# Another issue order, paired first q matmuls and PSUM places written out in a fused attention, FFT and MLP kernel

## The chip, the cores and the metric

The kernel runs on one core of a Trainium2 chip. The time is device microseconds of that core from the start of a launch to its end, the median of several executions. Every execution starts with all inputs in HBM, the weights among them as 64-bit patterns that the kernel decodes itself.

## What is computed

The reference, cut to what matters (four batches, four heads, sequence 1088, head dimension 32, r = 8, so 64 features):

```python
def phi(x):                                   # S1, S2: (8, 32)
    a = einsum('rd,bhsd->bhsr', S1, x)
    b = einsum('rd,bhsd->bhsr', S2, x)
    return einsum('bhsi,bhsj->bhsij', a, b).reshape(..., 64)
kv  = einsum('bhsf,bhsd->bhfd', phi(k), v);  z = sum(phi(k), axis=s)
x   = einsum('bhsf,bhfd->bhsd', phi(q), kv) / (einsum('bhsf,bhf->bhs', phi(q), z) + 1e-6)
u   = x + real(fft(fft(x, axis=seq), axis=channel))       # x as (4, 1088, 128)
un  = (u - mean(u)) / sqrt(var(u) + 1e-6)                 # over the 128 channels
y   = u + relu(un @ w_ch1) @ w_ch2                        # 128 -> 512 -> 128
h   = relu(y @ w_in)                                      # 128 -> 1024
out = (h * sigmoid(conv3(h))) @ w_out                     # 3 taps along the sequence
```

## The kernel before

The channels (or four heads times 32) lie on the 128 partitions, the sequence on the free axis. Each of the four batches goes through five stages: `load_attn`, `attn`, `fft`, `moe1` (normalization and the first MLP) and `moe2` (the second). The code is written stage by stage, but no instruction is issued where it stands: `Program` records each call, and `issue` (line 153) sends them out in the order of the table `ORDER`, so that batches and stages overlap and each engine's queue is fixed by the table. All profile lines carry the line number of the recorder (L157) for that reason, and groups are told apart by their tiles. No scheduler reorders anything after that; an instruction waits in its engine's queue for the semaphores of its operands.

What the change and the steps of the prediction touch:

- `load64` (line 182) loads a 64-bit weight (`raw`) on SP's queue and decodes it: one ACT operation and six on DVE, on the tile `em`. It is called for `srep` (the two 8x32 matrices S1, S2), `w1`, `w2`, `win` in two halves, `cw` and `wout` in two halves.
- From `s_rep` come `sab_sb` (eight DVE copies, weights for the factors `a` and `b`) and `sq_sb` (eight ACT copies, the same with each row repeated eight times).
- `idle` (line 235): 24 matmuls on zeros that write a tile nobody reads. Each fp32 matmul makes two records in the trace, so 24 are 48 records.
- `consts_fft` (line 274): `mats_sb` on SP's queue; `tab_hi`, `tab_lo`, `tab_end` (2.6 MB of cosines and sines) on POOL's queue, each behind a one-column copy that reads `q_sb[0]`, so that no table is fetched before the first q is there.
- `attn`: for batch 0 (`P["sq"]`) the features of q come from 12 matmuls of 128 rows by 364 columns against `sq_sb`, an ACT copy and a DVE product for each two. The other batches take `qab_ps<-q,sab_sb` (4 matmuls), and spread the result through DRAM. For k: 9 matmuls `kab_ps`, a copy `kb`, six products `kp` on DVE. Then `kv_ps`: 36 matmuls that write one of two column halves (`kp_0` the one, `kp_1` the other), an ACT copy `vk` for each half and one transposing matmul `kvt_ps` (batches 0, 1, 3: `P["kvt"]`), or 18 matmuls `kv_ps<-v,kp` that need no transposing (batch 2). `kv` and `z` are copied out of PSUM by DVE (lines 404, 405). `den` (24 matmuls of 32 columns), its reciprocal `rd`, and `num` (6) follow; batch 0 spreads `rd` by the matmuls `rb`.
- `fft`: `xe` and `xo` (even and odd part), four DVE operations `parts`, the matmuls `p_ps`, then `spec` against the tables.
- `q_sb`, `k_sb` and `v_sb` have one buffer each, so the load of batch 1's q waits for the last matmul that reads batch 0's.
- PSUM: `bank` gives a tile of one bank from one of two pools, five banks for `mm` and three for `acc`.

Of the kernel before, what the change touches and what calls it, by code (L numbers as in the profile page):

```python
# [9 lines left out]
F32 = mybir.dt.float32  # L10
# [5 lines left out]
ALU = mybir.AluOpType  # L16
# [3 lines left out]
P = dict(near=(0,), kvt=(0, 1, 3), hs=(), hlo=4, xb=2, sq=(0,), rpe=(0,), up=(0,), mo=12, hid=7, idle=24)  # L20
BANKS = {"mm": 5, "acc": 3}
# [8 lines left out]
HALF = 544  # L30
RT = 273
# [107 lines left out]
class Program:  # L139
# [13 lines left out]
    def issue(self):  # L153
        assert sorted(ORDER) == list(range(len(self.ops)))
        for i in ORDER:
            fn, args, kw = self.ops[i]
            fn(*args, **kw)  # L157
# [576 lines left out]
```

## Time and profile before

| | us |
|---|---|
| median of 3 executions | 260.36 (259.74 to 261.38) |
| profiled execution, span of its instructions | 259.4 |
| median minus that span | 0.96 |
| PE busy | 250.8 (97%) |
| DVE busy | 234.4 (90%) |
| ACT busy | 183.6 (71%) |

The profiled execution's own time is known by its span, from the first to the last instruction on the core. Busy shares are over that span. PE's busy time counts a matmul until its modelled end, and matmuls overlap, so that 97% means that PE is nearly always given work and not that it could do none in less time. In the chain that ended last PE has 81% of the span, DVE 10%, transfers 4%.

### The profile page before, as it was taken

Reading aid. Unit: us, or ns where it says so; the run is one execution under the profiler, and the core shown is the slowest. Engines: PE = TensorE matmul, PEld = TensorE weight load, DVE = VectorE, ACT = ScalarE, POOL = GpSimd, SP = SyncE. Lnnn points to the kernel's source line nnn. Section 1 sums busy time; section 2 is a strip of 40 time slices with the busy share of each in tenths; the row PEclk is TensorE's granted clock in tenths of the full one; section 3 lists DMA queues with packets and bytes.
Section 4 is the critical chain, followed back from the end, with each engine's and each line's share of the span. In section 5 each row is a group of like instructions: output and inputs, shape, how many; then the busy total and the mean of one; then the engine's idle time right before and its main releaser. Section 6 shows DMA issues by size and latency. Waiting matters only on the chain.

```text
span 259.4 us, 4622 instructions
## 1 busy us (share of the span) xinstructions
PE 250.8 (97%) x1812; PEld 198.5 (77%) x1812; DVE 234.4 (90%) x356; ACT 183.6 (71%) x330; POOL 6.5 (2%) x15
## 2 busy tenths in 40 slices
PE   7799999999999999999989999999999999999994
PEld 7566679876979887778878877678988877877652
DVE  2588999988999999989999999999999998999970
ACT  3342433972986847873788978996999998999822
POOL 1400000030000000000000000000000000000000
PEclk9799999999999999999999999999999999999999
DMA  7999299385568204184303001500000050000202
GB/s 225 329 402 284 85 304 236 115 228 179 123 147 195 75 24 122 42 175 131 86 4 114 11 0 15 137 0 0 3 0 29 9 143 0 0 3 1 85 0 86
DMA packets 11557, 26.87 MB, mean 104 GB/s; under 512 B 2224, under 2 KB 6832, under 8 KB 11280
## 3 DMA queue, kind: packets, MB, share of 16 engines
q1 hardware_dynamic: 11136, 23.92, 32.9%
q0 software_dynamic: 400, 2.67, 2.9%
q8 instruction: 14, 0.23, 0.4%
q14 instruction: 7, 0.06, 0.1%
HBM read 23.27 MB, written 3.31 MB: 102 GB/s over the span
## 4 chain that ended last, share of the span: by engine, by line
PE 81%; DVE 10%; DMA 4%; ACT 2%; issue 1%; SPq 0%; ACTq 0%; DVEq 0%
PE z L157 25%; PE acc L157 20%; PE ch L157 10%; PE qab_ps L157 5%; DMA q<-qT 4%; PE spec L157 4%; PE kv_ps L157 4%; DVE t L157 4%; PE p_ps L157 3%; PE num L157 3%; PE kab_ps L157 2%; PE cen L157 2%; ACT t L157 1%; PE var L157 1%; DVE ch L157 1%
## 5 line engine op out<-in xcount | busy, mean ns | idle before, releaser
L157 DVE SCALAR_TENSOR_TENSOR t<-h,cw_sb,t 128x1087 f32<-128x1087 f32 x64 | 83.8, 1340 | 0.9 <-ACT t L157 0.4
L157 PE MATMUL acc<-t,wo_sb 128*128 128x364 f32 (+1 forms) x192 | 69.3, 469 | 0.0
L157 ACT ACTIVATE h<-z 128x364 f32<-128x364 f32 (+1 forms) x96 | 41.0, 472 | 15.2 <-PE z L157 14.8
L157 DVE TENSOR_TENSOR t<-t,h 128x1088 f32<-128x1088 f32 (+2 forms) x34 | 40.9, 1217 | 4.6 <-ACT t L157 4.5
L157 PEld LDWEIGHTS acc<-t,wo_sb 128*128 128x128 f32 x192 | 34.3, 189 | 9.1 <-DVE t L157 0.6
L157 ACT ACTIVATE t<-h,cw_sb 128x1088 f32<-128x1088 f32 x32 | 38.4, 1204 | 0.4
L157 ACT ACTIVATE t<-t 128x1088 f32<-128x1088 f32 (+2 forms) x34 | 35.5, 1058 | 4.3 <-DVE t L157 4.3
L157 PE MATMUL z<-yh,win_hi 128*128 128x364 f32 (+1 forms) x96 | 37.2, 414 | 0.0
L157 PE MATMUL z<-yl,win_hi 128*128 128x364 f32 (+1 forms) x96 | 34.1, 366 | 0.2 <-DVE yl L157 0.2
L157 PE MATMUL z<-yh,win_lo 128*128 128x364 f32 (+1 forms) x96 | 34.1, 359 | 0.0
L157 PE MATMUL ch<-hid,w_sb 128*128 128x364 f32 (+1 forms) x96 | 33.3, 469 | 0.0
L157 ACT ACTIVATE hid<-z 128x364 f32<-128x364 f32 (+1 forms) x48 | 21.3, 474 | 7.4 <-PE z L157 7.1
L157 PEld LDWEIGHTS ch<-hid,w_sb 128*128 128x128 f32 x96 | 17.3, 189 | 6.6 <-ACT hid L157 0.5
L157 PEld LDWEIGHTS z<-yh,win_hi 128*128 128x128 f32 x96 | 17.7, 189 | 5.1 <-ACT h L157 1.0
L157 PEld LDWEIGHTS z<-yh,win_lo 128*128 128x128 f32 x96 | 18.1, 189 | 3.1
L157 PEld LDWEIGHTS z<-yl,win_hi 128*128 128x128 f32 x96 | 18.0, 189 | 2.6 <-DVE yl L157 0.5
L157 PE MATMUL z<-uh,w_hi 128*128 128x364 f32 (+1 forms) x48 | 19.2, 410 | 0.0
L157 PE MATMUL z<-uh,w_lo 128*128 128x364 f32 (+1 forms) x48 | 16.9, 358 | 0.0
L157 PE MATMUL z<-ul,w_hi 128*128 128x364 f32 (+1 forms) x48 | 16.4, 359 | 0.0
L157 PE MATMUL p_ps<-mats_sb,parts 128*32 128x128 f32 (+1 forms) x160 | 15.4, 276 | 0.7 <-ACT pe L157 0.7
L157 PEld LDWEIGHTS p_ps<-mats_sb,parts 128*32 128x32 f32 (+1 forms) x160 | 13.2, 142 | 2.2 <-ACT pe L157 0.9
L157 DVE TENSOR_TENSOR kp<-kab_ps,kb 121x512 f32<-121x512 f32 (+1 forms) x24 | 12.2, 546 | 0.5 <-ACT kb L157 0.5
(118 smaller groups left out, 389.3 us busy)
## 6 DMA issues: line engine op xcount, KB each, us to landing
qa<-qd SPq DMA_DIRECT2D x6, 546.0 KB
qb<-qd SPq DMA_DIRECT2D x12, 273.0 KB
v<-va SPq DMA_DIRECT2D x4, 594.0 KB
q<-qT SPq DMA_DIRECT2D x4, 546.0 KB, 6.4
k<-kT SPq DMA_DIRECT2D x4, 544.5 KB
x<-rrd SPq DMA_DIRECT2D x12, 136.5 KB, 4.1
y<-rtd SPq DMA_DIRECT2D x3, 544.0 KB
out<-r SPq DMA_DIRECT2D x8, 182.0 KB
```

The lines of the kernel that those rows point to most:

```text
L157: fn(*args, **kw)
```

## The change

It has six parts. (1) SP's queue starts with `srep`, q and k of batch 0, and `w1` comes behind them; the second half of `win` is fetched ahead of the first; POOL's copies that hold the tables back read `v_sb[0]` in place of `q_sb[0]`. (2) Batch 0's q features: 12 matmuls of 64 rows each in place of 12 of 128 rows (the other 64 rows of those weights are zeros); row halves 0 and 64 take turns, and the matmuls of a pair write different banks. (3) All eight PSUM banks are one tile `every`, and `HOMES` says for each use which bank it has; the 12 `wide` slots get written-out places too. (4) Batch 2 takes the transposed form of kv too. (5) The copies of `kv` and `z` go from DVE to ACT (16 instructions). (6) `xe` and `xo` become one tile `xeo`, and the four `parts` operations of a batch two. `idle` goes from 24 to 15 matmuls, all of them ahead of the first q matmul. And the whole table `ORDER` is another one.

```diff
-P = dict(near=(0,), kvt=(0, 1, 3), ..., sq=(0,), rpe=(0,), up=(0,), mo=12, hid=7, idle=24)
-BANKS = {"mm": 5, "acc": 3}
+P = dict(near=(0,), kvt=(0, 1, 2, 3), ..., sq=(0,), rpe=(0,), up=(0,), mo=12, hid=7, idle=15)
...
-    def bank(nm, tag="mm"):
-        return ps.tile([128, 512], F32, tag=tag, bufs=BANKS[tag], name=nm)
+    every = ps.tile([128, 8, 512], F32, name="every") if HOMES else None
+    def bank(nm):
...
+        return every[:, int(next(homes["bank"]))]
...
         for t, src in ((tab_hi, thi), (tab_lo, tlo), (tab_end, tend)):
-            G.tensor_copy(t[:, 0, 0:1], q_sb[0][:t.shape[0], 0:1])
+            G.tensor_copy(t[:, 0, 0:1], v_sb[0].rearrange("p t h d -> p (t h d)")[:t.shape[0], 0:1])
             G.dma_start(t, src)
...
-            for hp in range(2):
-                for i in range(3):
-                    c = slice(i * 364, (i + 1) * 364)
-                    pab = [bank(f"qab_ps{b}_{hp}_{i}_{s}", "acc") for s in range(2)]
-                    for s in range(2):
-                        w = sq_sb[:, s, 2 * hp:2 * hp + 2].rearrange("p h i j -> p (h i j)")
-                        T.matmul(pab[s][:, :364], w, qt[:, c], start=True, stop=True)
+            for i in range(3):
+                c = slice(i * 364, (i + 1) * 364)
+                pab = {}
+                for s in range(2):
+                    for hp in range(2):
+                        r = slice(64 * hp, 64 * hp + 64)
+                        w = sq_sb[r, s, 2 * hp:2 * hp + 2].rearrange("p h i j -> p (h i j)")
+                        pab[s, hp] = bank(f"qab_ps{b}_{hp}_{i}_{s}")
+                        T.matmul(pab[s, hp][:, :364], w, qt[r, c], start=True, stop=True)
...
-            V.tensor_copy(kv[r, :, 32 * h2:32 * h2 + 32], kvv[h2][:, :, 0:32])
-            V.tensor_copy(zz[r, ...], kvv[h2][:, :, 32])
+            A.copy(kv[r, :, 32 * h2:32 * h2 + 32], kvv[h2][:, :, 0:32])
+            A.copy(zz[r, ...], kvv[h2][:, :, 32])
...
-        for i, (src, op, eng) in enumerate(
-            ((xe, ALU.add, V), (xe, ALU.subtract, V), (xo, ALU.subtract, V), (xo, ALU.add, V))
-        ):
-            eng.tensor_tensor(parts[:, i], src[:, 0:RT], src[:, HALF:RT - 2:-1], op=op)
+        for to, op in ((parts[:, 0:4:3], ALU.add), (parts[:, 1:3], ALU.subtract)):
+            V.tensor_tensor(to, xeo[:, :, 0:RT], xeo[:, :, HALF:RT - 2:-1], op=op)
```

The first place where the order differs is SP's queue at the start. `raw` is a weight's buffer, `q0`, `k0`, `v0` are batch 0's inputs, `q1`, `k1` batch 1's. Before:

```order
L157 DMA raw0_110<-w1 128x512
L157 DMA raw0_78<-srep 128x16
L157 DMA q0_109<-qT 128x1092
L157 DMA k0_107<-kT 128x1089
L157 DMA raw0_115<-win 128x512
L157 DMA mats_sb_93<-mats 128x896
L157 DMA v0_108<-va 128x1188
L157 DMA raw0_113<-w2 128x512
L157 DMA k1_258<-kT 128x1089
L157 DMA q1_260<-qT 128x1092
```

Now:

```order
L164 DMA raw0_79<-srep 128x16
L164 DMA q0_109<-qT 128x1092
L164 DMA k0_107<-kT 128x1089
L164 DMA raw0_110<-w1 128x512
L164 DMA mats_sb_93<-mats 128x896
L164 DMA raw512_116<-win 128x512
L164 DMA v0_108<-va 128x1188
L164 DMA q1_181<-qT 128x1092
L164 DMA raw0_112<-w2 128x512
L164 DMA k1_179<-kT 128x1089
```

`w1` has gone from the first place to the fourth, the other half of `win` stands there, and batch 1's q has come ahead of `w2` and of its k.

The second place is PE's queue at the start, up to the first `kv` matmuls. Before, where the tiles `qab_ps`, `kab_ps` and `kv_ps` have names of their own:

```order
L157 MATMUL idle_88<-still_87 128x128 x13
L157 MATMUL qab_ps0_0_0_0_134<-q0_109,sq_sb_81 128x364
L157 MATMUL qab_ps0_1_0_0_140<-q0_109,sq_sb_81 128x364
L157 MATMUL kab_ps0_0_128<-sab_sb_80,k0_107 121x64 x5
L157 MATMUL qab_ps0_1_0_1_141<-q0_109,sq_sb_81 128x364
L157 MATMUL qab_ps0_1_1_0_142<-q0_109,sq_sb_81 128x364
L157 MATMUL kab_ps0_0_128<-sab_sb_80,k0_107 121x64 x3
L157 MATMUL qab_ps0_0_1_0_136<-q0_109,sq_sb_81 128x364
L157 MATMUL qab_ps0_0_2_0_138<-q0_109,sq_sb_81 128x364
L157 MATMUL kab_ps0_1_129<-sab_sb_80,k0_107 121x64
L157 MATMUL qab_ps0_0_1_1_137<-q0_109,sq_sb_81 128x364
L157 MATMUL qab_ps0_1_2_0_144<-q0_109,sq_sb_81 128x364
```

Now, where every result is a bank of `every` and the operands tell what a row is (`q0,sq_sb` the features of q, `sab_sb,k0` those of k, `q1,sab_sb` batch 1's q, `kp0,v0` batch 0's kv):

```order
L164 MATMUL every_75<-still_88 128x128 x15
L164 MATMUL every_75<-q0_109,sq_sb_82 128x364 x12
L164 MATMUL every_75<-sab_sb_81,k0_107 121x64 x9
L164 MATMUL every_75<-em0_111,mats_sb_93 128x512
L164 MATMUL every_75<-q1_181,sab_sb_81 64x273
L164 MATMUL every_75<-kp0_0_127,v0_108 33x64 x14
L164 MATMUL every_75<-q1_181,sab_sb_81 64x273
L164 MATMUL every_75<-kp0_0_127,v0_108 33x64 x4
L164 MATMUL every_75<-kp0_1_128,v0_108 33x64 x18
L164 MATMUL every_75<-q1_181,sab_sb_81 64x273
```

The q matmuls stand in one row of twelve, the nine of k behind them; batch 1's q has come ahead of the kv matmuls, and those stand in runs, 18 of `kp0_0` (14 and 4) and then 18 of `kp0_1`, where before the two take turns.

The third place is batch 1's kv on PE. Before, a part of it (the pattern goes on to the end):

```order
L157 MATMUL kv_ps1_274<-kp1_0_272,v1_259 33x64
L157 MATMUL kv_ps1_274<-kp1_1_273,v1_259 33x64
L157 MATMUL kv_ps1_274<-kp1_0_272,v1_259 33x64
L157 MATMUL kv_ps1_274<-kp1_1_273,v1_259 33x64 x2
L157 MATMUL kv_ps1_274<-kp1_0_272,v1_259 33x64
L157 MATMUL kv_ps1_274<-kp1_1_273,v1_259 33x64
```

Now, between the last `spec` matmuls of batch 0 and its `moe1`:

```order
L164 MATMUL every_75<-kp1_1_190,v1_180 33x64
L164 MATMUL every_75<-q2_245,sab_sb_81 64x273
L164 MATMUL every_75<-kp1_1_190,v1_180 33x64 x3
L164 MATMUL every_75<-q2_245,sab_sb_81 64x273
L164 MATMUL every_75<-kp1_0_189,v1_180 33x64 x2
L164 MATMUL every_75<-kp1_1_190,v1_180 33x64 x6
L164 MATMUL every_75<-q2_245,sab_sb_81 64x273
L164 MATMUL every_75<-kp1_0_189,v1_180 33x64
L164 MATMUL every_75<-kp1_1_190,v1_180 33x64 x4
L164 MATMUL every_75<-q2_245,sab_sb_81 64x273
L164 MATMUL every_75<-kp1_0_189,v1_180 33x64 x15
L164 MATMUL every_75<-kp1_1_190,v1_180 33x64 x4
```

The halves stand in runs of up to 15 here, with batch 2's q (`q2`) in between. Over batches 1 to 3, 76 of the 108 kv matmuls follow one of the same half, where before it is 11 of 72 (batch 2 had the other form).

On DVE, the decode of `win`'s first half (`em0_115`) and the end of that of `w2` have gone from ahead of batch 0's `xe` and `parts` to behind its `spec`. The matmuls that wait for PE's own semaphore were 15 and are none.

## Rows read from the trace of the kernel before

**Rows 1.** The page's head and part 1: busy time, share, instructions.
```profile
span 259.4 us, 4622 instructions
...
PE 250.8 (97%) x1812; PEld 198.5 (77%) x1812; DVE 234.4 (90%) x356; ACT 183.6 (71%) x330; POOL 6.5 (2%) x15
```

**Rows 2.** Windows: width, busy us by engine (count), clock, DMA.
```profile
0.00:40.00 40.00, 35.81 (x325) 26.98 (x326) 29.99 (x81) 15.78 (x41) 3.71 (x11) 0.96 0.82 272
40.00:250.00 210.00, 209.12 (x1471) 168.23 (x1470) 202.82 (x273) 166.01 (x287) 2.75 (x4) 1.00 0.28 74
```

**Rows 3.** Timeline of the first 40 us: start, length, engine, instruction, idle before it.
```profile
0.72 0.40 SPq L157 DMA_DIRECT2D raw<-w  x1
...
1.17 4.97 PE L157 MATMUL idle<-still 128*128 128x128 f32 x26 [1.17 <-DVE still L157]
1.19 0.41 SPq L157 DMA_DIRECT2D raw<-srep  x1
...
4.71 0.77 ACT L157 ACTIVATE em<-raw 128x16 f32<-128x16 f32 x2 [2.71 <-DMA raw<-srep]
...
6.00 0.18 DVE L157 TENSOR_TENSOR s_rep<-em 128x16 f32<-128x16 f32 x1
...
6.27 1.52 ACT L157 COPY sq_sb<-s_rep 32x64 f32<-32x64 f32 x6 [0.79 <-DVE s_rep L157]
...
8.17 1.34 PE L157 MATMUL qab_ps<-q,sq_sb 128*128 128x364 f32 x2 [2.03 <-DMA q<-qT]
...
12.15 1.44 PE L157 MATMUL qab_ps<-q,sq_sb 128*128 128x364 f32 x4
...
14.62 1.88 DVE L157 TENSOR_TENSOR kp<-kab_ps,kb 121x512 f32<-121x512 f32 x3 [0.47 <-ACT kb L157]
...
22.57 0.30 PE L157 MATMUL kv_ps<-kp,v 121*33 121x64 f32 x2 [0.35 <-ACT vk L157]
...
24.97 1.17 PE L157 MATMUL den<-qa,z 128*32 128x91 f32 x48
...
28.70 0.69 DVE L157 SCALAR_TENSOR_TENSOR em<-raw,em 128x512 f32<-128x512 uint32 x1
...
31.60 2.12 PE L157 MATMUL kab_ps<-sab_sb,k 128*121 128x64 f32 x18
...
34.35 1.14 PE L157 MATMUL qab_ps<-q,sab_sb 128*64 128x273 f32 x8 [0.64 <-DMA q<-qT]
...
38.86 0.39 PE L157 MATMUL spec<-tab_hi,ph 128*128 128x274 f32 x1
```

**Rows 4.** Windows of 2 us round the first `q` matmuls.
```profile
8.00:10.00 2.00, 1.83 (x4) 1.06 (x5) 1.90 (x7) 0.45 (x1) 1.57 (x4) 0.60 0.84 262
10.00:12.00 2.00, 2.00 (x11) 1.72 (x10) 0.43 (x2) 0.71 (x3) 1.42 (x3) 0.55 1.07 411
12.00:14.00 2.00, 2.00 (x14) 1.53 (x13) 0.98 (x2) 0.37 (x1) 0.00 (x0) 1.00 1.02 410
```

**Rows 5.** PE timeline, `kv_ps` in its two forms.
```profile
44.02 2.21 PE L157 MATMUL kv_ps<-kp,v 121*33 121x64 f32 x72
...
69.68 1.45 PE L157 MATMUL kv_ps<-v,kp 121*128 121x66 f32 x12
```

**Rows 6.** PE timeline at 120 us: five `kv_ps` records of one half.
```profile
120.20 0.44 PE L157 MATMUL kv_ps<-kp,v 121*33 121x64 f32 x5
```

**Rows 7.** Groups by line and form: count, busy us, mean ns, idle before.
```profile
L157 PE MATMUL kv_ps<-kp,v 121*33 121x64 f32 x216 | 8.0, 220 | 0.3 <-ACT vk L157 0.3
...
L157 DVE COPY kv<-kvt_ps 64x64 f32<-64x64 f32 x6 | 1.3, 217 | 0.1
```

**Rows 8.** DMA issues: count, KB each, median us from issue to landing.
```profile
q<-qT SPq DMA_DIRECT2D x4, 546.0 KB, 6.4
...
tab_end<-tend POOLq DMA_DIRECT2D x1, 411.0 KB, 13.9
...
rtd<-rt SPq DMA_DIRECT2D x3, 34.0 KB, 1.5
```

More of the change, by code (lines that the diff above doesn't have):

```diff
@@ L18 @@
 DRAM = bass.MemoryType.DRAM
-P = dict(near=(0,), kvt=(0, 1, 3), hs=(), hlo=4, xb=2, sq=(0,), rpe=(0,), up=(0,), mo=12, hid=7, idle=24)
-BANKS = {"mm": 5, "acc": 3}
+P = dict(near=(0,), kvt=(0, 1, 2, 3), hs=(), hlo=4, xb=2, sq=(0,), rpe=(0,), up=(0,), mo=12, hid=7, idle=15)
 LEAST, MOST = np.array([896 << 20, (1151 << 20) - 1], np.int32).view(np.float32).tolist()
@@ L47 @@
 ORDER = [
[74 rows of a table removed]
-]
[74 rows of a table added]
+]
+HOMES = {
+    "bank": (
+        "064557205141037623552734101354301031414143402555472001264327104137567232532507174722313014560546474454373746755643604777"
+        "536454432363231346156574656607457030274331235232515661553176135162555126332351064366557736361256322150236133443524550721"
+        "2403500305642450432034502422"
+    ),
+    "wide": "012391948a175b8324107a2685475046b24b751980a36255b704a62781b5097134639a6a94519a42859b043978",
+}
 class Queue:
@@ L153, in issue @@
     def issue(self):
-        assert sorted(ORDER) == list(range(len(self.ops)))
-        for i in ORDER:
+        assert not ORDER or sorted(ORDER) == list(range(len(self.ops)))
+        for i in ORDER or range(len(self.ops)):
             fn, args, kw = self.ops[i]
@@ L168, in tile_fwd, with place @@
     ln = ctx.enter_context(tc.tile_pool(name="ln", bufs=1))
-    mo = ctx.enter_context(tc.tile_pool(name="mo", bufs=P["mo"]))
+    mo = ctx.enter_context(tc.tile_pool(name="mo", bufs=1))
     dr = ctx.enter_context(tc.tile_pool(name="dr", bufs=2, space=DRAM))
-    ps = ctx.enter_context(tc.tile_pool(name="ps", bufs=5, space=PSUM))
-    def bank(nm, tag="mm"):
-        return ps.tile([128, 512], F32, tag=tag, bufs=BANKS[tag], name=nm)
+    ps = ctx.enter_context(tc.tile_pool(name="ps", bufs=1, space=PSUM))
+    homes = {kind: iter(places) for kind, places in HOMES.items()}
+    def place(pool, shape, dtype, kind, bufs, nm):
+        if kind in homes:
+            return pool.tile(shape, dtype, tag=kind + next(homes[kind]), bufs=1, name=nm)
+        return pool.tile(shape, dtype, tag=kind, bufs=bufs, name=nm)
+    every = ps.tile([128, 8, 512], F32, name="every") if HOMES else None
+    def bank(nm):
+        if every is None:
+            return ps.tile([128, 512], F32, tag="bank", bufs=8, name=nm)
+        return every[:, int(next(homes["bank"]))]
     def lo_of(eng, dst, src, hi):
@@ L179, in slot @@
     def slot(nm):
-        return mo.tile([128, WIDE], F32, tag="wide", name=nm)
+        return place(mo, [128, WIDE], F32, "wide", P["mo"], nm)
     def load64(src, n, use, then=lambda o, w, x: None):
@@ L235, in tile_fwd @@
     if P["idle"]:
-        idle = bank("idle", "acc")
+        idle = bank("idle")
         for i in range(P["idle"]):
@@ L314, in attn @@
             for i in range(2):
-                p = bank(f"qab_ps{b}_{i}", "mm")
+                p = bank(f"qab_ps{b}_{i}")
                 for j in range(2):
@@ L332, in attn @@
         kb = at.tile([KT, NKT, NH, RK], F32, tag="kb", name=f"kb{b}")
-        kp0 = bank(f"kab_ps{b}_0", "mm")
-        kp1 = bank(f"kab_ps{b}_1", "mm")
+        kp0 = bank(f"kab_ps{b}_0")
+        kp1 = bank(f"kab_ps{b}_1")
         for t in range(NKT):
@@ L360, in attn @@
         kv, zz = kvz[b % 2]
-        kv_ps = bank(f"kv_ps{b}", "mm")
+        kv_ps = bank(f"kv_ps{b}")
         if b in P["kvt"]:
@@ L376, in attn @@
                 A.copy(vk[r, :], kv_ps[r, :128])
-            kv_ps = bank(f"kvt_ps{b}", "mm")
+            kv_ps = bank(f"kvt_ps{b}")
             T.matmul(kv_ps[:, :128], vk, eye_sb, start=True, stop=True)
@@ L392, in attn @@
         if b in P["sq"]:
-            for hp in range(2):
-                for i in range(3):
-                    c = slice(i * 364, (i + 1) * 364)
-                    pab = [bank(f"qab_ps{b}_{hp}_{i}_{s}", "acc") for s in range(2)]
-                    for s in range(2):
-                        w = sq_sb[:, s, 2 * hp:2 * hp + 2].rearrange("p h i j -> p (h i j)")
-                        T.matmul(pab[s][:, :364], w, qt[:, c], start=True, stop=True)
-                    A.copy(qa[hp][:, c], pab[0][:, :364])
-                    V.tensor_tensor(qa[hp][:, c], qa[hp][:, c], pab[1][:, :364], op=ALU.mult)
+            for i in range(3):
[7 more added lines that the diff above has]
+                        T.matmul(pab[s, hp][:, :364], w, qt[r, c], start=True, stop=True)
+                for hp in range(2):
+                    A.copy(qa[hp][:, c], pab[0, hp][:, :364])
+                    V.tensor_tensor(qa[hp][:, c], qa[hp][:, c], pab[1, hp][:, :364], op=ALU.mult)
         for h2 in range(2):
             r = slice(64 * h2, 64 * h2 + 64)
-            V.tensor_copy(kv[r, :, 32 * h2:32 * h2 + 32], kvv[h2][:, :, 0:32])
-            V.tensor_copy(zz[r, DJ - 1 + DJ * h2:DJ + DJ * h2 + ZW + 2 * DJ:ZW + 2 * DJ], kvv[h2][:, :, 32])
+            A.copy(kv[r, :, 32 * h2:32 * h2 + 32], kvv[h2][:, :, 0:32])
+            A.copy(zz[r, DJ - 1 + DJ * h2:DJ + DJ * h2 + ZW + 2 * DJ:ZW + 2 * DJ], kvv[h2][:, :, 32])
         for hp in range(0 if b in P["sq"] else 2):
             V.tensor_tensor(qa[hp], qa[hp], qb[hp], op=ALU.mult)
-        den = bank(f"den{b}", "mm")
+        den = bank(f"den{b}")
         for hp in range(2):
@@ L427, in attn @@
             for c in range(4):
-                p = bank(f"rb{b}_{c}", "mm")
+                p = bank(f"rb{b}_{c}")
                 for j in range(DJ):
@@ L439, in attn @@
         for i in range(3):
-            n = bank(f"num{b}_{i}", "mm")
+            n = bank(f"num{b}_{i}")
             for hp in range(2):
@@ L453, in fft @@
         x = xs.pop(b)
-        xe = ff.tile([128, HALF + 1], F32, tag="xe", name=f"xe{b}")
-        xo = ff.tile([128, HALF + 1], F32, tag="xo", name=f"xo{b}")
+        xeo = ff.tile([128, 2, HALF + 1], F32, tag="xeo", name=f"xeo{b}")
         fw, bw = x[:, 0:HALF + 1], x[:, SEQ:HALF - 1:-1]
-        V.tensor_tensor(xe, fw, bw, op=ALU.add)
-        V.tensor_tensor(xo, fw, bw, op=ALU.subtract)
+        V.tensor_tensor(xeo[:, 0], fw, bw, op=ALU.add)
+        V.tensor_tensor(xeo[:, 1], fw, bw, op=ALU.subtract)
         parts = ff.tile([128, 4, RT], F32, tag="parts", name=f"parts{b}")
-        for i, (src, op, eng) in enumerate(
-            ((xe, ALU.add, V), (xe, ALU.subtract, V), (xo, ALU.subtract, V), (xo, ALU.add, V))
-        ):
-            eng.tensor_tensor(parts[:, i], src[:, 0:RT], src[:, HALF:RT - 2:-1], op=op)
+        for to, op in ((parts[:, 0:4:3], ALU.add), (parts[:, 1:3], ALU.subtract)):
+            V.tensor_tensor(to, xeo[:, :, 0:RT], xeo[:, :, HALF:RT - 2:-1], op=op)
         ph = ff.tile([128, 8, D], F32R, tag="ph", name=f"ph{b}")
@@ L588, in moe2 @@
         yh, yl = ys.pop(b)
-        acc = [bank(f"acc{b}_{i}", "acc") for i in range(3)]
+        acc = [bank(f"acc{b}_{i}") for i in range(3)]
         hs, ts = {}, {}
```

148 rows, old and new, of the table ORDER are left out of this document.

## The prediction

> **What bounds the kernel now.** I read the page's busy shares first: PE 97% and DVE 90% of 259.4 us [rows 1]. A share over the whole span hides stages, so the windows came next [rows 2]. From 40 to 250 us PE is busy 209.12 of 210 us and DVE 202.82: PE gives the pace, DVE follows close behind, and a gain there must take work off PE's queue without adding to DVE's. From 0 to 40 us it is otherwise: PE is busy 35.81 us, but part of that is work on zeros and part ran at a low clock. So the timeline of that stretch was read, link by link, for what the first `spec` at 38.86 us waits for [rows 3]. The chain is: the DMA of `srep`, on which ACT sat idle 2.71 us until 4.71; `s_rep` at 6.00; the `sq_sb` copies from 6.27; the first q matmul at 8.17, in front of which PE idled 2.03 us for q; the matmuls of q and k; the `kp` products from 14.62 (0.63 us each for the long ones); the last kv matmuls at 22.57; `den` at 24.97; `spec` at 38.86. In the windows behind the 2.03 us gap the granted clock is 0.60 and 0.55, so TensorE ran partly at its lower level of 1.2 GHz there, and 1.00 (2.4 GHz) from 12 us on [rows 4].
>
> **The start, step by step.** All steps are set against the profiled execution; the median lies 0.96 us above its span (260.36 against 259.4).
>
> *srep first.* Before, its DMA is issued at 1.19 us behind `w1` and ACT starts on it at 4.71, 3.5 us later [rows 3]. Issued in `w1`'s place at 0.72 it is used by 4.2 us if it takes as long; without 512 KB ahead of it less, with the 1.5 us that the 34 KB of `rtd` take [rows 8] as the other end, so 2.2. I take 2.6, near that end, since nothing stands ahead of it now. From there to the end of `s_rep` it is 1.47 us (4.71 to 6.18), and eight `sq_sb` copies at 0.25 us (six took 1.52) end at 6.2. q is issued at 1.65 and lands after 6.4 us [rows 8], so at 8.05; issued 0.46 us earlier and with 512 KB less ahead (1.25 us at the 411 GB/s of rows 4) it lands at 6.3 or before.
>
> *The clock.* 15 `idle` matmuls are 30 records; 26 took 4.97 us, from 1.17 [rows 3], so 30 end near 6.6. The q matmuls then follow with no gap: first q at 6.6 rather than 8.17, and the 3.83 busy us of the windows at 0.60 and 0.55 become some 2.2. The 11 idle matmuls that stood further back are gone; they filled gaps, so leaving them out is costed at nothing, unless the clock falls in such a gap: the only fall in these rows follows 2.03 us without work, and for another I keep up to 1 us in the range.
>
> *q and k.* Four full-height records start at 12.15 and the k matmuls behind them at 13.43, so 0.32 each [rows 3]. 24 such records are 7.7 us. As 64-row pairs that run side by side they are 12 times 0.32, 3.9 us. No row shows two row halves of q at once. The ends are 3.9 and 7.7; the nearest row is that of kv, whose two column halves in turn take 28 ns a record (2.21 us less a last one of 0.22, over 71 steps [rows 5, 7]), against 55 ns for five of one half ((0.44 - 0.22) / 4 [rows 6]). Two parts of the array do work side by side, so I take 3.9. The Trainium skill, "TensorE: Matmul & The Clock Gate", Part 3 (Measured speedup vs the span model), has four row groups at 3.07 times one and not at four; by an estimate from that the pairs would cost some 5 us, and the sum 1.2 more. So q ends at 10.5, and the nine k matmuls behind it (18 records, 2.12 us [rows 3]) at 12.6.
>
> *kp and kv.* DVE, which waits 0.47 us for the copy `kb` on ACT, then has four long products (0.63), two of a quarter of the size (0.3, an estimate) and, between them, two decode steps of `w1` at 0.69 [rows 3]: 12.6 + 0.5 + 2.5 + 0.6 + 1.4 = 17.6. The first run of kv (18 matmuls) goes while this lasts, the second stands behind it: 36 records at 55 ns, 2.0, to 19.7 with the last one's length. Before, kv ends at 22.87: **-3.2 us**, and `den` comes at 21.8 (before, 24.97).
>
> *From den to spec.* Before, 13.9 us, with 12 decode steps on DVE between the x products, `xe`, `xo` and `parts`; now 8 stand there. Four fewer, at up to 0.69 each, are up to 2.8 us, if DVE is the late one there; if it is PE, nothing. PE also loses 1.14 us of `qab_ps` (batch 2's q) from this stretch [rows 3]. I take -2.2, ends 0 and -3.5. So `spec` comes at 33.5 in place of 38.86, **-5.4 us**; with the ends of each step, -3 to -7. The tables, whose DMAs now start when v is there (3.2 MB into the queue, near 10 us at 400 GB/s), land after at most 13.9 us [rows 8], at 24, so `spec` covers them.
>
> **What is added behind the start.** (1) The `qab_ps` of batch 2 comes after `spec` now: +1.1, PE work of the dense stretch. (2) Batch 2's kv: 36 records at (1.45 - 0.22) / 11 = 0.112 are 4.0 us [rows 5], and become 72 at 28 ns and a transposing pair of 128 columns (0.3, an estimate from 364 columns at 0.32): 2.3, **-1.7**. (3) Runs of one half: 76 of 108 kv matmuls follow one of their own half, 65 more than before, and 65 x 2 records x 27 ns are +3.5 if each such step costs 55 ns in place of 28; nothing if PE takes a later matmul of the free half meanwhile, or other work stands between. Rows 6 are nearest to the full price; as batch 2's q and other matmuls stand between some, I take **+2.4**. (4) 15 matmuls no longer wait for PE's own semaphore: at most the 0.9 us that PE idles from 40 to 250 [rows 2]; I take **-0.5**. (5) DVE: 16 copies of at most 0.217 us [rows 7] go to ACT, which is busy 71%: some -3; two operations fewer a batch in `parts`; and nine decode steps (of 24, 15 are left ahead of `spec`) come into this stretch: up to 6.2. 202.82 + 3 stays under PE's 210, so 0 (end: +1.5). The one tile `every` could make waits between banks; the order shows none, so 0. Sum: **+1.3**, ends -1.5 and +4.
>
> The tail (last `acc` matmuls, copy, DMA) is the same: 0. So 259.4 - 5.4 + 1.3 = 255.3, and with 0.96 for the median 256.3 us.
>
> **The rivals.** *Eaten lead.* From 40 us PE and DVE have 0.9 and 7 us to spare [rows 2]. If `den` to `spec` stays 13.9 us because PE is the late one (+2.2) and the runs cost their full 3.5 (+1.1), it ends at 259.6, no change. For it: PE at 209 of 210, and a DVE that gets nine decode steps more. Against: PE's work in the first 40 us does shrink. A rule of the Trainium skill would lead there: "TensorE: Matmul & The Clock Gate", Part 3 (The mechanism), says that matmuls start and end strictly in order. Then every run costs 55 ns a step, as rows 6 show.
>
> *Slower: batch 1's q holds up kv.* In PE's queue `qab_ps` of q1 stands ahead of all kv matmuls. q1 shares q0's buffer, so its DMA can be issued only after the last q matmul, near 10.5, and then shares the DMA engines with tables, `w2` and v: 4 MB are under way. It lands after 6.4 us (the median of q) to 13.9 (`tab_end`, issued in the same crowd before) [rows 8]: 16.9 to 24.4. The first kv run has 2 us of slack before the second can begin, so up to 15.5 it costs nothing, and beyond that each us comes on the end: at 16.9 +1.4, at 24.4 +8.9, which is 265.2. It turns the kernel slower than 262.96 from a landing at 22 us. Against: 13.9 is the last of three tables in a row, and q1 is one transfer of 546 KB on the other queue; at half of 400 GB/s it takes under 3 us, which is why the forecast has none of it.
>
> *Pairs that do nothing.* If 64-row matmuls run one after the other, q ends 3.8 us later; kv moves by as much, and the end is 260.1: no change.
>
> *More gain.* If PE works past the runs (-2.4), `den` to `spec` is short (-1.3) and PE's 0.9 idle us go (-0.4), it ends at 252.
>
> **How the numbers follow.** A measurement of this kernel can tell about 1% from no change, so faster is below 257.8 and slower above 263.0. The forecast, 254 to 258.5, has 0.50 (0.45 of it below 257.8); more gain 0.15; the eaten lead, or a small wait for q1, 0.17; pairs that do nothing 0.04; q1's long wait, or several waits of the new order that add up to it, 0.14. So faster is 0.60, same 0.26, slower 0.14. The range leaves out the long wait and the tip of the gain: 251.5 to 262.
>
> **What would show it.** Right: ACT's first `em` before 4.3 us; q matmuls with no idle time ahead of them and a granted clock of 1.00 from 6 to 12 us; the 24 q records in under 5 us; the last kv of batch 0 near 20; `spec` between 32 and 35.5; PE as busy as before from there on. Wrong: PE idle ahead of q1's `qab_ps` near 15 us with the DMA as releaser; q records at 0.32 each; kv in runs at 55 ns a record with nothing between; or DVE at 100% from 40 us on, with PE waiting for it.

## The result and the profile after

The changed kernel takes 262.70 us (median of 14 runs, 262.12 to 265.12) against 261.73 us for the kernel before, run beside it (14 runs, 259.74 to 265.38). The ratio is 1.0064, 95% interval 1.0038 to 1.0090: 0.6% slower, where 256.3 us had been forecast. The ratio is formed from the faster runs of each kernel, so it is not the quotient of the two medians. The profiled execution's span is 262.8 us, 3.4 us more than in [rows 1].

That execution took 264.58 us, and its mean granted clock is 0.992. One other of the 14 has 0.992 too (265.12 us); the remaining twelve have 0.998 to 1.000 and took 262.12 to 263.13 us. What the clock does in the rows below is therefore not part of the median.

Head and part 1 of the page of the kernel after:

```profile
span 262.8 us, 4654 instructions
...
PE 253.9 (97%) x1832; PEld 204.5 (78%) x1832; DVE 231.9 (88%) x332; ACT 186.0 (71%) x348; POOL 5.7 (2%) x15
```

PE's share has not moved, though its busy time is 3.1 us more; DVE's is 2.5 us less, where the sum had some 3. By windows (columns as in [rows 2]):

```profile
0.00:40.00 40.00, 36.64 (x339) 30.41 (x339) 28.02 (x75) 14.84 (x41) 3.52 (x11) 0.96 0.88 278
40.00:250.00 210.00, 207.98 (x1466) 168.83 (x1466) 198.46 (x252) 167.58 (x301) 2.17 (x4) 1.00 0.29 70
```

PE still gives the pace from 40 to 250 us. It idles 2.0 of the 210 us there, where before it was 0.9.

The start of the kernel after, from the timeline (for PE, every result is a bank of `every`, and the operands tell the group: `q,sq_sb` the features of q, `q,sab_sb` batch 1's q, `kp,v` kv, `qa,z` den, `mats_sb,parts` p_ps, `tab_hi,ph` spec):

```profile
1.17 6.01 PE L164 MATMUL every<-still 128*128 128x128 f32 x30 [1.17 <-DVE still L164]
...
2.37 0.22 ACT L164 ACTIVATE em<-raw 128x16 f32<-128x16 f32 x1 [0.37 <-DMA raw<-srep]
...
7.11 4.16 PE L164 MATMUL every<-q,sq_sb 64*128 64x364 f32 x24
...
11.31 0.33 SPq L164 DMA_DIRECT2D q<-qT  x1
...
15.06 0.44 PE L164 MATMUL every<-q,sab_sb 128*64 128x273 f32 x1
...
18.08 2.03 PE L164 MATMUL every<-kp,v 121*33 121x64 f32 x33 [0.35 <-ACT vk L164]
...
21.65 1.87 PE L164 MATMUL every<-qa,z 128*32 128x91 f32 x48
...
30.22 4.84 PE L164 MATMUL every<-mats_sb,parts 128*128 128x128 f32 x40 [1.08 <-DVE parts L164]
...
34.99 0.40 PE L164 MATMUL every<-tab_hi,ph 128*128 128x272 f32 x1
```

Against [rows 3]: ACT starts on `srep` at 2.37 in place of 4.71; the first q matmul is at 7.11, right behind the idle ones; 24 q records take 4.16 us; batch 1's q was fetched at 11.31 and its matmul at 15.06 waited for no DMA; den starts at 21.65, where 21.8 was forecast. Then den takes 1.87 us where it took 1.17, `p_ps` 4.84 us behind a wait of 1.08, and `spec` starts at 34.99: 3.9 us ahead of before, not 5.4. Windows of the kernel after from 28 us on:

```profile
28.00:30.00 2.00, 1.14 (x11) 1.00 (x10) 1.97 (x4) 0.37 (x1) 0.00 (x0) 1.00 0.32 128
30.00:32.00 2.00, 1.78 (x8) 1.81 (x9) 2.00 (x6) 0.00 (x0) 0.00 (x0) 0.53 0.84 207
32.00:34.00 2.00, 2.00 (x15) 1.88 (x14) 0.85 (x2) 0.42 (x1) 0.00 (x0) 0.62 1.03 416
34.00:36.00 2.00, 2.00 (x32) 1.80 (x28) 1.58 (x3) 1.56 (x4) 0.00 (x0) 1.00 0.87 326
```

Behind that wait the granted clock is 0.53 and 0.62, TensorE's lower level (1.2 GHz) for most of the four us; before, it was 1.00 in all windows between 12 and 40 us. Over 262.8 us such a fall alone (2 us at 0.53, 2 us at 0.62) takes 0.0065 off the mean, so the twelve executions at 0.998 and more have no room for it.

What is lost behind `spec` shows in PE's groups. Of the kernel after, by form (count, busy us, mean ns):

```profile
L164 PE MATMUL every<-kp,v 121*33 121x64 f32 x288 | 17.0, 220 | 0.6 <-ACT vk L164 0.6
...
L164 PE MATMUL every<-qa,z 128*32 128x91 f32 x192 | 10.4, 245 | 0.0
...
L164 PE MATMUL every<-mats_sb,parts 128*32 128x128 f32 x96 | 7.8, 277 | 0.0
...
L164 PE MATMUL every<-sq,one_v 128*32 128x68 f32 x96 | 3.3, 226 | 0.0
```

And of the kernel before, the three of them that are not in [rows 7]:

```profile
L157 PE MATMUL den<-qa,z 128*32 128x91 f32 x192 | 6.6, 244 | 0.0
...
L157 PE MATMUL p_ps<-mats_sb,parts 128*32 128x128 f32 x96 | 5.5, 275 | 0.7 <-ACT pe L157 0.7
...
L157 PE MATMUL var<-sq,one_v 128*32 128x68 f32 x96 | 2.0, 226 | 0.0
```

The mean length of a record is the same (220 and 245 ns; 244 before), but they overlap less: den 10.4 us in place of 6.6, the 32-column `p_ps` 7.8 in place of 5.5, `var` 3.3 in place of 2.0, kv 17.0 for 288 records where 216 took 8.0. To see what each group costs PE, I summed over its records behind the first `spec` the time from its start to the start of the next matmul, in us (groups that alternate with each other go together):

| group | before | after | with turns (below) |
|---|---|---|---|
| kv, both forms | 8.2 | 10.4 | 7.8 |
| den | 4.6 | 6.6 | 3.6 |
| p_ps | 7.0 | 8.4 | 7.3 |
| var | 1.8 | 3.1 | 2.0 |
| z and acc of moe2 | 105.3 | 105.9 | 106.5 |
| z and ch of moe1 | 56.2 | 57.1 | 58.7 |
| all others | 33.5 | 32.3 | 32.9 |
| sum, first `spec` to last matmul | 216.6 | 223.9 | 218.7 |

From `spec` to the end the kernel after needs 7.3 us more than before, and 6.9 of it stand in kv, den, p_ps and var. All four write halves or quarters of the array's columns, and in all four the new order has matmuls of one part in runs. Counted within each group in the two order tables, 50 of the 96 den matmuls follow one of their own quarter (before, 2), 14 of the 48 of the 32-column `p_ps` (before, 2) and 26 of the 48 of var (before, none).

### The profile page after: what moved, and what is told of

It reads as the page before. It is cut to its first block, busy times and chain, and to the rows that moved or that the text cites. A ratio compares the mean times of both kernels' runs of the same rounds, so it can differ in the third digit from the quotient of the medians.

```text
span 262.8 us, 4654 instructions
## 1 busy us (share of the span) xinstructions
PE 253.9 (97%) x1832; PEld 204.5 (78%) x1832; DVE 231.9 (88%) x332; ACT 186.0 (71%) x348; POOL 5.7 (2%) x15
## 4 chain that ended last, share of the span: by engine, by line
PE 80%; DVE 10%; ACT 4%; DMA 4%; issue 1%; DVEq 0%; ACTq 0%; SPq 0%
PE every L164 80%; DVE t L164 4%; DMA y<-rtd 3%; DVE every L164 1%; ACT t L164 1%; DVE kp L164 1%; ACT L164 1%; DMA rtd<-rt 1%; DVE xeo L164 1%; DVE em L164 1%; ACT h L164 0%; DVE x L164 0%; DVE ul L164 0%; DVE yl L164 0%; DVE u L164 0%
## 5 line engine op out<-in xcount | busy, mean ns | idle before, releaser
L164 PE MATMUL every<-t,wo_sb 128*128 128x364 f32 (+1 forms) x192 | 66.5, 469 | 0.0
L164 ACT ACTIVATE h<-every 128x364 f32<-128x364 f32 (+1 forms) x96 | 40.6, 472 | 9.1 <-PE every L164 7.8
L164 PEld LDWEIGHTS every<-t,wo_sb 128*128 128x128 f32 x192 | 34.8, 189 | 13.5 <-DVE t L164 1.1
L164 PE MATMUL every<-yh,win_hi 128*128 128x364 f32 (+1 forms) x96 | 34.6, 380 | 1.7 <-ACT yh L164 1.7
L164 PE MATMUL every<-hid,w_sb 128*128 128x364 f32 (+1 forms) x96 | 32.0, 468 | 0.0
L164 PE MATMUL every<-yh,win_lo 128*128 128x364 f32 (+1 forms) x96 | 31.8, 346 | 0.0
L164 PE MATMUL every<-yl,win_hi 128*128 128x364 f32 (+1 forms) x96 | 30.4, 351 | 0.0
L164 ACT ACTIVATE hid<-every 128x364 f32<-128x364 f32 (+1 forms) x48 | 20.9, 474 | 4.3 <-PE every L164 4.2
L164 PE MATMUL every<-mats_sb,parts 128*32 128x128 f32 (+1 forms) x160 | 18.7, 290 | 1.1 <-DVE parts L164 1.1
L164 PE MATMUL every<-uh,w_hi 128*128 128x364 f32 (+1 forms) x48 | 18.5, 406 | 0.0
```

## The experiments

My theory after the result: a run of matmuls for one part of the array leaves the other parts idle, and PE pays it, in four groups and not in kv alone; beside that, in the profiled execution, the fall of the clock at 30 us. The main rival: the lead was lost to waits on ACT and DVE (copies moved to ACT, decode steps moved back), and the runs cost little.

**Turns in all four groups, on the changed kernel.** Each matmul of the groups is noted with its part; `issue` then puts the k-th matmuls of all parts behind one another, at the place of the last of them, so that nothing is issued ahead of what it needs:

```diff
+                        nc.note = (f"kv{b}", hp)          # den: c; p_ps: r; var: c
                         T.matmul(
...
+            for k in range(0, n, RUN):                    # RUN = 1: turns
+                turn = [pair for tile in sorted(rows) for pair in rows[tile][k:k + RUN]]
+                last = max([last] + [at for at, _ in turn])
+                extra.setdefault(last, []).extend(i for _, i in turn)
```

> The changed kernel, but the matmuls of kv (two column halves), den and var (four column quarters each) and the 32-column p_ps (three quarters) take turns between the parts of the array in PE's queue. Theory (runs in one part are paid in full on PE, in den, p_ps and var as well as in kv): kv 15.0 to about 8.1 us of PE's stream, den 8.4 to 5, p_ps and var 8 to 5; PE paces, so 8 to 11 us less: about 253. Rival (the lead of the start was lost to waits on ACT and DVE, runs cost little): kv and den get shorter but PE waits instead, 260 or more.

254.79 us; ratio to before 0.9725 (0.9703 to 0.9746). By form, with turns:

```profile
L187 PE MATMUL every<-kp,v 121*33 121x64 f32 x288 | 12.2, 220 | 0.0
...
L187 PE MATMUL every<-qa,z 128*32 128x91 f32 x192 | 5.4, 244 | 0.0
...
L187 PE MATMUL every<-mats_sb,parts 128*32 128x128 f32 x96 | 4.7, 274 | 0.0
...
L187 PE MATMUL every<-sq,one_v 128*32 128x68 f32 x96 | 2.2, 226 | 0.1
```

kv is down from 17.0 to 12.2, den from 10.4 to 5.4, p_ps from 7.8 to 4.7, var from 3.3 to 2.2. The timeline of the same run:

```profile
19.36 1.16 PE L187 MATMUL every<-qa,z 128*32 128x91 f32 x48
...
27.48 3.03 PE L187 MATMUL every<-mats_sb,parts 128*128 128x128 f32 x40 [1.15 <-DVE parts L187]
...
30.43 0.39 PE L187 MATMUL every<-tab_hi,ph 128*128 128x272 f32 x1
```

den takes 1.16 us, and `spec` starts at 30.43, 8.4 us ahead of before. The theory holds: without the runs the time is some 8 us under the 262.70 (253 was expected). The wait ahead of `p_ps` is still there (1.15), and the granted clock is 1.00 in all windows round it.

**Runs, on the kernel before.** The same code with `RUN = 4`.

> The kernel before, but with kv, den, p_ps and var matmuls in runs of up to four of one part of the array. Theory: kv of batches 0, 1 and 3 from 28 to near 50 ns a record (+4.5), den, p_ps and var +4 together: 267 to 271. Rival (runs cost little): 261 to 263.

271.35 us, ratio 1.0358 (1.0327 to 1.0390). But kv hardly took part. Timeline, batch 1's kv and den:

```profile
45.42 2.64 PE L180 MATMUL kv_ps<-kp,v 121*33 121x64 f32 x72
...
64.23 2.18 PE L180 MATMUL den<-qa,z 128*32 128x91 f32 x48
```

72 kv records in runs of four matmuls take 2.64 us, against 2.21 in turns [rows 5], while den takes 2.18 in place of 1.17. The span of the profiled execution is 268.4 us, 9.0 more than before. `spec` starts 1.4 us later (40.26 against 38.86). Behind it, summed as in the table above, kv costs 8.7 us (before, 8.2), den 7.3 (4.6), `p_ps` 9.6 (7.0) and var 4.2 (1.8): 8.2 us more, where the whole stretch takes 7.6 more. So the price stands in the groups that were put into runs, and the three in quarters pay most of it.

**kv in two runs of 18, on the kernel before** (`RUN = 18`, kv alone).

> The kernel before with kv of batches 0, 1 and 3 in two runs of 18 matmuls (36 records) each; runs of four had left kv as it was (11.4 to 11.6 us). Theory (PE starts matmuls of a free part past some waiting records, but not past 36): kv near 52 ns a record, 3 to 5 us more of PE's stream: 264 to 267. Rival (runs of any length cost kv little, den, p_ps and var cost all): 261 to 262.5.

264.62 us, ratio 1.0096 (1.0063 to 1.0129). Batch 1's kv:

```profile
44.22 4.02 PE L180 MATMUL kv_ps<-kp,v 121*33 121x64 f32 x72
```

4.02 us, 54 ns a record: the full price of one half. Behind `spec` kv costs 3.1 us more than before, and the span is 3.4 us longer. So runs of 18 are paid in full, runs of four for about a quarter (2.64 and 4.02 us against 2.21).

**Turns of two, on the changed kernel** (`RUN = 2`).

> As the turns in all four groups, but two matmuls (four records) of one part, then two of the next. If PE starts a matmul of a free part past four waiting records: as with turns of one, 254.8. If it holds the order: the second matmul of each two waits for the first and holds up the next part, kv near 42 ns a record: 258 to 260.

255.68 us, ratio 0.9785 (0.9724 to 0.9846); the interval overlaps that of turns of one. Batch 1's kv:

```profile
37.13 1.98 PE L187 MATMUL every<-kp,v 121*33 121x64 f32 x64
```

64 records take 1.98 us, 28 ns a record, as with turns of one (there 62 records in a row take 1.98). In strict order eight records would take six steps of 55 ns, 41 ns a record. So PE does start a matmul of a free half past waiting ones. Over all batches kv's steps add up to 9.6 us, with turns of one to 10.1.

**Turns in kv alone.**

> The changed kernel with turns in kv alone; den, p_ps and var stay in runs. Theory (every group pays its own runs): kv 15.0 to 10.1 us of PE's stream as with turns in all four groups, the others unchanged: about 257.5 to 258.5. Rival (kv is all that counts): 255, as with turns in all four.

259.48 us, ratio 0.9930 (0.9901 to 0.9958). Of the 7.9 us that turns in all four gain on the changed kernel, kv brings 3.2 (262.70 to 259.48), and den, p_ps and var the other 4.7. kv's own steps fall by 4.9 us (15.0 to 10.1), so not every us that PE saves there comes on the end, and the time lies above the range expected.

**Turns on the kernel before.**

> The kernel before with turns in kv, den, p_ps and var. Theory (before already takes turns nearly everywhere; what turns cost the change is not what it gained elsewhere): 260 to 261.5, so that the rest of the change is worth 5 to 7 us against it. Rival (the gain of turns is a gain on any order): 256 or less.

260.57 us, ratio 0.9971 (0.9923 to 1.0019): no gain that can be told from none. If the two add up, the parts of the change without its runs are worth what lies between 0.9971 and 0.9725, about 2.5% or 6.4 us.

**Idle matmuls at 29 us.** Five matmuls on zeros ahead of batch 0's first `p_ps`, into a bank that is free there.

```diff
+        order[at:at] = [i for i, note in enumerate(self.notes) if note == ("warm", 0)]
```

> The changed kernel with five idle matmuls ahead of batch 0's first p_ps matmul, into a bank that is free. Theory (the fall of the granted clock to 0.53 and 0.62 from 30 to 34 us follows PE's wait of 1.1 us there, and idle matmuls had kept the clock before): p_ps records of batch 0 at 112 instead of 213 ns, clock 1.00 throughout, 1.3 to 1.6 us less: about 261.2. Rival (the clock falls whatever PE does there, or the chain is on DVE): no change, 262.7.

261.95 us; 0.75 us under the changed kernel by the medians, ratio to before 1.0001 (0.9982 to 1.0020). PE's timeline:

```profile
29.14 1.33 PE L167 MATMUL every<-still 128*128 128x128 f32 x10
30.38 3.26 PE L167 MATMUL every<-mats_sb,parts 128*128 128x128 f32 x40
33.57 0.39 PE L167 MATMUL every<-tab_hi,ph 128*128 128x272 f32 x1
```

The same 40 records take 3.26 us in place of 4.84, and the clock is 1.00 throughout: that is the price of the lower clock, 1.6 us, in an execution where it falls. `spec` then starts at 33.57. But twelve of the 14 executions of the changed kernel had no fall to save, so the 0.75 us by the medians must have another cause, which no run shows. That idle matmuls keep the clock up is not shown either: all ten executions here have a mean of 0.998 or more, against twelve of 14 without them.

**The 64-row pairs undone** (`r = slice(0, 128)`).

> The changed kernel with batch 0's q matmuls on all 128 rows again, in the same places. Theory (64-row matmuls run in pairs, 24 records in 4.1 us): 24 records take 7.6 us, everything behind is 3 to 3.5 us later: about 266. Rival (the kp products on DVE or the kv runs hide it): under 264.

274.55 us, ratio 1.0475 (1.0451 to 1.0499), far beyond both. Timeline:

```profile
7.14 7.51 PE L164 MATMUL every<-q,sq_sb 128*128 128x364 f32 x24
...
12.56 0.84 POOL L164 DMA_DIRECT2D tab_end<-tend  x1
...
14.68 0.33 SPq L164 DMA_DIRECT2D q<-qT  x1
...
23.68 0.69 PE L164 MATMUL every<-q,sab_sb 128*64 128x273 f32 x1 [5.53 <-DMA q<-qT]
```

The q matmuls cost 7.51 us in place of 4.16, as expected. But batch 1's q shares their buffer and is fetched behind the last of them, now at 14.68, behind the tables, of which the first is issued at 12.56. It is there 9 us later, and PE, which has it ahead of kv, waits 5.53 us; the clock is 0.50 to 0.53 from 20 to 26 us. This is the prediction's rival of a late q1, made to happen.

**The tables fetched when the first q lands**, with turns (POOL's copies read `q_sb[0]`, their six instructions behind q's DMA).

> The kernel with turns, but the tables are fetched when the first q is there, as before the change, so that batch 1's q stands behind 2.6 MB. Theory: batch 1's q lands near 21 to 24 us, PE waits for it ahead of all kv matmuls: 259 to 262. Rival (the queues share, it lands in time): 255.

261.76 us, ratio 1.0002 (0.9967 to 1.0037), 7 us more than with the tables held:

```profile
5.50 0.84 POOL L193 DMA_DIRECT2D tab_end<-tend  x1
...
10.86 0.33 SPq L193 DMA_DIRECT2D q<-qT  x1
...
19.65 1.18 PE L193 MATMUL every<-q,sab_sb 128*64 128x273 f32 x4 [5.01 <-DMA q<-qT]
```

PE waits 5.01 us for q1, and the clock is 0.50 from 16 to 24 us, in that wait and after it.

**w1 first on SP's queue again**, with turns.

> The kernel with turns, but w1 is fetched ahead of srep, q and k, as before the change. Theory (srep, q and k first gave the start 1.5 to 2 us): first q matmul near 8.2 to 8.7 us in place of 7.1, granted clock below 1 for a while behind that gap: 256.5 to 258. Rival (another link sets the start, the place of w1 is worth nothing): 254.8.

256.74 us (the middle of three runs; a fourth took 260.03), ratio 0.9825 (0.9753 to 0.9898), against 0.9725: the intervals lie just apart. By these times srep first is worth 2.0 us, by the spans of the profiled executions (254.4 and 253.1) 1.3.

```profile
4.79 0.22 ACT L191 ACTIVATE em<-raw 128x16 f32<-128x16 f32 x1 [2.79 <-DMA raw<-srep]
...
7.96 4.63 PE L191 MATMUL every<-q,sq_sb 64*128 64x364 f32 x24 [0.36 <-issue]
```

**The copies of kv and z on DVE again**, with turns (`V.tensor_copy`).

> The kernel with turns, with the copies of kv and z on DVE again. Theory (PE paces and DVE has room for 3 us): 254.3 to 255.5, no change. Rival (DVE is the late one between den and the next stage): 256 to 258.

260.74 us, ratio 0.9963 (0.9926 to 1.0000): 6 us worse, where I expected nothing. DVE's time is not what was short. In this order the `z` copy stands in DVE's queue ahead of the products `qa`:

```profile
18.76 0.33 DVE L187 COPY z<-every 64x2 f32<-64x2 f32 x2 [2.23 <-PE every L187]
19.13 0.98 DVE L187 TENSOR_TENSOR qa<-qa,every 128x364 f32<-128x364 f32 x2
...
20.94 1.14 PE L187 MATMUL every<-qa,z 128*32 128x91 f32 x42 [0.88 <-DVE qa L187]
```

DVE idles 2.23 us for kvt with `qa` queued behind, den then waits 0.88 us for `qa`, and `spec` starts at 33.84 in place of 30.43. In this execution the clock falls as well (0.50 from 30 to 32 us), but the six runs with a mean of 0.998 or more take 259.74 to 261.07 us, so the 6 us are not the clock's. Behind `spec` 3.4 us more are lost in the later batches; which waits make them up is not shown.

**12 idle matmuls at the start in place of 15**, with turns.

> The kernel with turns and 12 idle matmuls at the start in place of 15. Theory (q and sq_sb are there by 6.0 to 6.3 us, the last idle matmuls hold the first q matmul up until 7.1): first q at 6.3 to 6.6, 254.1 to 254.6. Rival (q lands at 7, or the clock falls in the gap): 254.8 to 256.5.

255.37 us, ratio 0.9745 (0.9711 to 0.9779): no change. In the profiled executions the first q matmul comes only 0.26 us earlier (6.59 against 6.85).

The version with turns beats both kernels: 254.79 us, 2.75% under before.

## Why the prediction was wrong

The step that failed is the third term of what is added behind the start, **"Runs of one half: 76 of 108 kv matmuls follow one of their own half"**. It counted kv and no other group, though the same new order puts den, p_ps and var, which write quarters, into runs as well. Behind `spec` these three cost 4.7 us more than before (2.1, 1.4, 1.3), and kv 2.2 more where kv's two terms together (+2.4 - 1.7) gave 0.7. That is 6.2 us beyond the forecast. The run with turns tells the two parts of kv apart: its runs cost 2.7 us (10.4 against 7.8), close to the +2.4, while the transposed form and all else brought 0.4 (8.2 to 7.8) and not 1.7. So the price that the term put on kv's runs was right; the groups that it left out were its fault. With turns the four groups lose 7.9 us, other groups gain 2.7, and the stretch behind `spec` goes from 223.9 to 218.7 us.

By spans the forecast was 255.3 us, and the middle execution of the changed kernel has 260.9: 5.6 us more, close to those 6.2. The rest of the 6.4 us between 256.3 and 262.70 is the term of 0.96 for the median. It sets a middle execution against the span of another, longer one; every run on record is 1.7 to 1.9 us longer than its own span.

The rival of the eaten lead quoted a rule of the Trainium skill, "TensorE: Matmul & The Clock Gate", Part 3 (The mechanism): matmuls start and end strictly in order. The runs bear that out by half: runs of 18 cost what strict order would (54 ns a record), runs of two and of four do not (28 and 34 ns). The eaten lead is half right too: the runs did eat it, through groups that this rival did not name and for more than its 259.6 us. But its other half, that `den` to `spec` stays at 13.9 us, did not come.

Point by point:

- *srep first*: right (2.37 against 2.6).
- *Clock at the start*: it is 1.00 from 6 to 14 us as said, but the 30 idle records took 6.01 us, and the first q matmul came at 7.11, not 6.6. The 1.6 us that this step was to save rest on one execution: of 52 runs of the kernel before beside the experiments, 41 have a mean granted clock of 0.997 or more, where the profiled one with its fall has 0.993, so most had no such fall to lose.
- *Pairs*: right in mechanism and size (4.16 against 3.9), and worth far more than their 3.3 us, since they also put q1's fetch ahead of the tables.
- *kp and kv*: den at 21.65 against 21.8.
- *From den to spec*: 13.3 us in the profiled execution, but 11.8 with the clock at 1.00 (21.80 to 33.57, with the idle matmuls at 29 us), against 11.7; den in runs stands in it with 0.7 us that the sum did not have.
- *Idle matmuls*: costed at nothing, with up to 1 us for a fall of the clock. In twelve of 14 executions no such fall came; in the profiled one `p_ps` took 1.6 us more.
- *q1 late*: rightly left out of the forecast, but by a small margin: q1's fetch was issued 1.8 us ahead of the first table (11.31 against 13.12).
- *Self-waits*: no gain seen; PE idles 1.1 us more from 40 to 250 us.
- *DVE*: right that it stays under PE (198.5 us busy), wrong that where the copies stand does not matter: with turns, 6 us hang on it.

Open: why the clock falls behind the wait at 29 us in the profiled execution (and, by its mean of 0.992, in one more) and not in the other twelve; what brings the 0.75 us of the idle matmuls there; and the 2.5 us more that moe1 has with turns (58.7 against 56.2). Not tried by themselves are the one tile `every` with its written-out places, the transposed kv of batch 2 and the two operations for `parts`; what each is worth is not shown.

## What to carry to other kernels

When matmuls use a half or a quarter of the array, the order among them is part of the cost: count, for every such group and not for the one that catches the eye, how many stand behind one of their own part. An order made without regard to that can lose here what it gains elsewhere; a pass that makes the parts take turns afterwards brought 3%. Where one buffer serves two batches, the last reader of the first sets when the second is fetched: what gets into the DMA queues just ahead of it decides microseconds. And before a fall of the clock in one profile is put into a sum, see by the mean granted clock of the other executions whether they had it.

## What the runs showed of the hardware

- fp32 records of 64 columns on one half of the array follow each other at 54 to 55 ns, on two halves in turns at 28. PE works past waiting matmuls of a busy half in runs of two (64 records in 1.98 us, no cost) and mostly in runs of four (72 records in 2.64 us in place of 2.21), not in runs of 18 (4.02).
- The granted clock can fall in one execution of a kernel and not in another: behind a wait of 1.08 us ahead of `p_ps` it was 0.53 in the profiled execution of the changed kernel, while twelve of 14 executions had no such fall; behind 1.15 us at the same place, with turns, it was 1.00.
- A 546 KB transfer issued 0.7 to 2.1 us behind three table transfers (2.6 MB) on another queue was there 9 us after its issue (14.68 to 23.68), and 8.8 us when issued 3.9 to 5.4 us behind them (10.86 to 19.65). Issued 1.8 us ahead of them it was there within 3.75 (11.31 to 15.06).
